# A stated order of 2997 steps: its first 950 rewritten with one filler product in place of ten, and three later steps moved forward

## The chip, the cores and the metric

The kernel runs on one core of a Trainium2 chip. The metric is the time of one execution on the device in microseconds. Before the change the median of three runs was 504.3 us (503.45 to 507.28). The core has five instruction streams that matter here: PE (TensorE, matrix products), DVE (VectorE), ACT (ScalarE), POOL (GpSimd) and SP (SyncE, which here only issues transfers). Each works off its own stream in order, and an instruction waits until what it needs is there.

## The reference

Two blocks follow one another. The first is a delta-rule recurrence over 768 tokens for 4 x 8 = 32 heads of width 48; the second, over the 384 features of each token, is a layer norm, a two-layer MLP with a relu, and a residual.

```python
k_n = k / (norm(k) + 1e-6)
state = zeros((B, H, D, D))
for t in range(S):
    y[:, :, t] = q[:, :, t] @ state
    v_old = state^T k_n[:, :, t]
    state = state + beta[t] * outer(k_n[:, :, t], v[:, :, t] - v_old)
x  = y as (B, S, H * D)                      # (4, 768, 384)
xn = (x - mean) / sqrt(var + 1e-6) * g_ln
out = x + relu(xn @ w_ch1) @ w_ch2           # 384 -> 1536 -> 384
```

All inputs and the output are float32.

## The kernel before

The 768 tokens are taken in 12 chunks of 64. Within a chunk the recurrence is turned into products: the products of the chunk's keys with one another (L772), the inverse of a triangular 64x64 matrix for each head, and then a handful of products with the state (`recur`, L970 to L1116), which is carried from chunk to chunk. The MLP of a chunk (`mlp`, L1275) follows its recurrence.

**The inverse.** For the first chunk it is built by doubling on PE (`first_inverse`, L643 to L750). For n = 1 to 5 there is a product E_n (L719) and a product Z_n (L738), each in two halves of 32 small products (half 0 and half 1 of the heads). Between E_n and Z_n a masked copy on DVE (`copy_predicated`, L728) puts E_n's result into place. Between Z_n and E_(n+1) DVE transposes the result (`nat`, L684) and ACT copies it (`back`, L678). For the other chunks the inverse is built on DVE in row blocks (L815 to L872, the pairs at L857 and L864) and joined by products on PE (`join`, L880 and after, products at L895 and L901).

**The recurrence of the first chunk.** u (product at L997, difference on DVE at L1002) and y (L1021) again come in two halves. ACT copies y into x (L1059), then the layer norm follows (statistics L941, normalisation L950, transposition on PE L1093, scaling by g_ln on ACT L1108). For later chunks the scaling by the reciprocal deviation is at L964 (DVE) and L966 (ACT).

**The MLP.** Chunk 0 is taken by halves of 128 columns (`by_halves`): first product L1323, second L1338. For chunks 1 to 3 the first product is at L1297, its relu on ACT at L1306. From chunk 4 the first product is replaced by fifteen smaller ones (`fifteen`, products L1218, sums L1234 to L1240). The second product is done by a scheme with seven products instead of eight (`seven`, L1399): products L1420, combinations of the relu's outputs on POOL (`comb`, L1407), sums on DVE (L1438).

**The weights** come as 64-bit words in pieces of 768 KB through ACT's queue (`fetch`), and are put together by two ACT instructions (L521, L529), one on DVE (L526) and one on POOL (`convert`, L539).

**What sets the order.** Building the kernel only records steps: `Line.add` stores for each of 2997 steps a function that issues its instructions, and which earlier steps it depends on. A string, `ORDER`, states in which order the steps are issued. `emit` reads it, asserts that a step's dependencies were issued, and calls the function. `in_this_order` then ties each engine's instructions into that order, and the transfers issued by SP and ACT into one order across both queues. No planner runs: what stands in `ORDER` is what each engine does. A step number a:b stands for a to b.

The letters z, y, x and w in `ORDER` are no steps of the computation. Each calls `zeros`, which issues one product of the identity with a broadcast column, 128 x 256, into the unused half of a bank; nothing reads it:

```python
    free = (f_[0], two[:, 0], by[:, 0], f_[1])

    def zeros(n):
        nc.tensor.matmul(free[n][:, 256:512], ident, ident[:, 0:1].to_broadcast([128, 256]))
```

Apart from them three products on zeros (`fill`, steps 71 to 73, L554) stand at the start.

The steps that the change names singly: 1026 and 1024 are two of chunk 2's first products of the MLP (L1297), 1027 and 1025 their relus (L1306); 993 is the layer-norm scaling on ACT (L966) and 994 the transposition on DVE behind it; 2953 and 2936 are two combinations on POOL (L1407) of the last chunk. In the front part: 59 is the load of g_ln, 69 and 386 are fetches of weight pieces, 360 is the second half of y of chunk 0.

Of the kernel before, what the change touches and what calls it, by code (L numbers as in the profile page):

```python
# [59 lines left out]
51 47 6 8 7 50 52 44 62 5 0 71:73 9:11 13 2 27 15 24 63 49 12 42 36 251 57 40 58 37 74 77 78 48 32 34 35 33 81 88 1 14 30 82 76 16 89 75 64 54 55 53  # L60
56 61 60 68 83 79 84 80 90 85 86 23 20 87 91 95 3 110 92 111 18 93 29 112 94 96 31 116 117 211 209 210 21 118 4 22 17 26 97 98 z 99 100 114 113 101
122 x 221 66 223 z 102 119 121 115 19 123:128 70 103 69 120 104 208 235 132 131 137 129 135 130 136 25 138 106 107 233 67 108 109 w 28 222 139 133 134
140 141 234 142:144 y 145 146 150 242 215 153 147 243 156 155 149 213 65 212 224 38 39 41 59 43 z 45 236 675 46 204 205 152 151 157 214 158 252 216
148 154 244 159 206 160:162 168 164 207 z 169 163 174 105 254 253 256 255 237 240 238 257 171:173 332 414 334 331 333 343 166 165 167 225 227 239 245
677 241 258 170 175 259 176 260 177 180 178 261 226 179 263 181 381 183 231 386 217 186 191 190 184 185 219 189 182 229 246 262 264:266 218 267:269 y
192 193 187 w 270:272 188 273 230 274:276 196 247 277 198 199 197 248 336 338 355 194 335 382 337 384 z 228 220 249 419 346 425 418 413 195 356 359
# [1585 lines left out]
```

## Time and profile before

| | us |
|---|---|
| median of three runs | 504.3 |
| lowest, highest | 503.45, 507.28 |
| profiled execution, its own time | 504.98 |
| its span in the profile | 502.8 |
| mean granted clock of PE in it | 0.981 |

Times in the profile count from the start of the span. A row of a timeline gives start, length, engine, line of the kernel, operation, tiles and shapes, and the number of like instructions in a row; in brackets stands the idle time of the engine ahead of it and what ended that. In a table by stretches each engine has its busy time and, in brackets, its number of instructions; then follow the granted clock of PE (1.00 is full), the share of the DMA engines and the bytes moved. A wait is put down to what came last. A product of fp32 leaves two records on PE where its tiles are 128 wide.

### The profile page before, as it was taken

The numbers are of one execution on the slowest core, as the hardware profiler recorded it, in microseconds if no ns is written. First come the engines' busy times: TensorE is split into PE (matmuls) and PEld (weight loads), VectorE is DVE, ScalarE is ACT, GpSimd is POOL, SyncE is SP. The second block draws the span as 40 slices with busy tenths as digits, with TensorE's granted clock in tenths as the row PEclk, the third lists the DMA queues.
The fourth block names the chain that finished last, engine by engine and source line by source line (L and its number), as shares of the span: only waits on it lengthen the run. The fifth ranks groups of instructions, "written<-read, shape, count | busy, mean of one in ns | idle before, by whom it ended". The sixth has DMA issues, their size and how long they took to land.

```text
span 502.8 us, 22213 instructions
## 1 busy us (share of the span) xinstructions
PE 488.1 (97%) x9624; PEld 445.3 (89%) x9624; DVE 348.5 (69%) x780; ACT 247.4 (49%) x620; POOL 277.8 (55%) x430
## 2 busy tenths in 40 slices
PE   8789999999999899999999999999999999999996
PEld 4567987689888898999999999999999999999996
DVE  6667998994889559886559898488899238143251
ACT  6767772623646234636544554436563347363230
POOL 5554468227873694629893561690642951645633
PEclk9976999999999999999999999999999999999999
DMA  9987987568656576448724525765234412111101
GB/s 166 308 153 187 252 200 103 78 178 130 84 91 108 186 128 112 68 78 214 153 36 66 108 48 162 145 92 83 75 68 126 94 22 60 44 50 47 26 15 31
DMA packets 196098, 54.99 MB, mean 109 GB/s; under 512 B 186077, under 2 KB 189405, under 8 KB 196001
## 3 DMA queue, kind: packets, MB, share of 16 engines
q1 hardware_dynamic: 189920, 40.58, 42.1%
q10 hardware_dynamic: 3872, 9.83, 6.3%
q0 software_dynamic: 2208, 3.17, 3.7%
q8 instruction: 75, 1.23, 1.0%
q14 instruction: 23, 0.18, 0.1%
HBM read 36.64 MB, written 16.91 MB: 107 GB/s over the span
## 4 chain that ended last, share of the span: by engine, by line
PE 81%; DVE 7%; DMA 4%; issue 3%; POOL 2%; ACT 1%; SPq 1%; DVEq 0%; ACTq 0%; POOLq 0%
PE f L1420 30%; PE f L1218 22%; PE f L1297 6%; DVE tmp L857 2%; DVE xb L864 2%; PE by L1021 2%; PE two L1014 2%; PE by L980 2%; PE two L980 2%; PE by L772 2%; PE f L1338 2%; PE two L1031 1%; PE two L772 1%; DMA gd<-gsb 1%; SPq L346 1%
## 5 line engine op out<-in xcount | busy, mean ns | idle before, releaser
L1407 POOL TENSOR_TENSOR h_all<-h_all 128x256 f32<-128x256 f32 x123 | 90.0, 744 | 131.6 <-PE f L1420 115.6
L1420 PE MATMUL f<-w_sb,h_all 128*128 128x192 f32 x492 | 108.1, 331 | 0.0
L1420 PE MATMUL f<-words,h_all 128*128 128x192 f32 x396 | 84.1, 330 | 1.7 <-ACT h_all L1306 1.4
L1420 PEld LDWEIGHTS f<-w_sb,h_all 128*128 128x128 f32 x492 | 81.7, 190 | 1.7 <-DVE o L1438 0.2
L857 DVE TENSOR_TENSOR tmp<-xb,gb 128x87 f32<-128x87 f32 (+21 forms) x186 | 74.1, 398 | 5.0
L864 DVE TENSOR_TENSOR xb<-xb,tmp 128x87 f32<-128x87 f32 (+21 forms) x186 | 72.3, 389 | 4.8
L1238 DVE TENSOR_TENSOR h_all<-h_all,f 128x512 f32<-128x512 f32 x96 | 63.4, 682 | 14.5 <-PE f L1218 13.3
L1420 PEld LDWEIGHTS f<-words,h_all 128*128 128x128 f32 x396 | 66.5, 190 | 3.2 <-ACT h_all L1306 1.5
L1297 PE MATMUL f<-xnt,w_sb 128*128 128x256 f32 x216 | 50.1, 382 | 0.0
L346 POOL DMA_DIRECT2D tb<-in_k_dram x64 | 41.8, 657 | 11.4 <-DVE kt L752 10.8
L1240 ACT ACTIVATE h_all<-h_all 128x512 f32<-128x512 f32 x48 | 28.4, 624 | 34.8 <-DVE h_all L1238 34.7
L1297 PEld LDWEIGHTS f<-xnt,w_sb 128*128 128x128 f32 x216 | 40.2, 190 | 5.1
L1234 ACT COPY h_all<-f 128x512 f32<-128x512 f32 x48 | 26.3, 590 | 34.9 <-PE f L1218 18.2
L1438 DVE TENSOR_TENSOR o<-f,x 128x192 f32<-128x192 f32 x33 | 11.6, 352 | 39.3 <-PE f L1420 22.8
L1218 PE MATMUL f<-words,w_sb 128*128 128x128 f32 x256 | 31.7, 276 | 0.0
L1218 PEld LDWEIGHTS f<-words,w_sb 128*128 128x128 f32 x256 | 30.0, 192 | 0.2
L1306 ACT ACTIVATE h_all<-f 128x256 f32<-128x256 f32 x36 | 13.4, 382 | 32.1 <-PE f L1297 31.9
L539 POOL TENSOR_TENSOR w_sb<-words 128x768 uint32<-128x768 uint32 (+1 forms) x11 | 15.2, 1387 | 19.9 <-DVE words L526 6.2
L1218 PE MATMUL f<-xnt,w_sb 128*128 128x128 f32 x192 | 25.4, 276 | 0.0
L1218 PEld LDWEIGHTS f<-xnt,w_sb 128*128 128x128 f32 x192 | 23.7, 192 | 0.1
L1438 DVE TENSOR_TENSOR o<-f,words 128x192 f32<-128x192 f32 x11 | 3.8, 349 | 25.4 <-PE f L1420 18.4
L1085 ACT ACTIVATE xnt<-xnt,g_sb 128x256 f32<-128x256 f32 x27 | 12.5, 499 | 16.4 <-DMA xnt<-xld 16.4
(250 smaller groups left out, 966.5 us busy)
## 6 DMA issues: line engine op xcount, KB each, us to landing
words<-in_moe_w_ch_dram ACTq DMA_DIRECT2D x10, 768.0 KB, 6.6
gd<-gsb SPq DMA_DIRECT2D x11, 512.0 KB, 3.8
v<-in_v_dram SPq DMA_DIRECT2D x24, 192.0 KB, 3.9
kr<-in_k_dram SPq DMA_DIRECT2D x46, 96.0 KB, 3.5
out_dram<-o SPq DMA_DIRECT2D x44, 96.0 KB, 2.4
xld<-xlt SPq DMA_DIRECT2D x9, 384.0 KB, 2.9
xnt<-xld SPq DMA_DIRECT2D x36, 96.0 KB, 3.1
gb<-gd SPq DMA_DIRECT2D x44, 64.0 KB, 3.2
```

The lines of the kernel that those rows point to most:

```text
L346: add(eng, cost, lambda: QUEUE[eng].dma_start(out=out_, in_=in_), r, w, bulk=n * ns / 16e3, **kw)
L857: lambda j=j, n=n, w=w, t=t: nc.vector.tensor_tensor(out=t, in0=xv[:, 0:n, j : j + 1].to_broadcast([np_, n, w]), in1=gv[:, j : j + 1, j + ...
L864: "DVE", dve(n * w), lambda t=t, rest=rest: nc.vector.tensor_tensor(out=rest, in0=rest, in1=t, op=ALU.subtract),
L980: nc.tensor.matmul(dst[half(e), hp, j], src[drows(hp), (e if n else key_half(c, hp, e)) * GP + j], s_all[drows(hp), e, j], start=(n == 0 o ...
L1218: nc.tensor.matmul(wide(p[:, 128 * n : 128 * n + 128]), w[n // 2][:, n % 2 * 128 : n % 2 * 128 + 128], r, start=start and n == 0, stop=Tru ...
L1234: add("ACT", act(512), lambda: nc.scalar.copy(o, p), pk, ok)
L1238: add("DVE", dve(512), lambda: nc.vector.tensor_tensor(out=o, in0=o, in1=p, op=op), pk, ok)
L1240: add("ACT", act(512), lambda: nc.scalar.activation(o, o, ACTF.Relu), [], ok)
L1297: nc.tensor.matmul(p[:, 0:TOK], w1_sb[:, t, f * 128 : (f + 1) * 128], xnt[:, t], start=(t == 0), stop=(t == KC - 1))
L1407: add(eng, cost, lambda: e.tensor_tensor(out=out_, in0=x, in1=y, op=op), r, w, port=2 if eng == "Pool" else 1, pr=-2)
L1420: lambda f=f, t=start and f == 0: nc.tensor.matmul(p[:, 0:D2], lhs(f), rhs[:, f], start=t, stop=(f == F2 - 1), skip_group_check=True),
L1438: lambda: e.tensor_tensor(out=out_, in0=a, in1=b_, op=ALU.add), r, w, pr=pr,
```

## The change

Only the string `ORDER` changes. No step is added or taken away; the letters are.

- The first 950 steps or so (up to about 140 us of the profile before) stand in another order, on all engines and all queues.
- The ten letters z x z w y z z y z z are replaced by a single y, between steps 97 and 98.
- Steps 1027, 1024 and 1025 stand ahead of 993 and 994 instead of behind them.
- Step 2953 stands ahead of 2936 instead of behind it.

All other lines of the string are the same in content, though its line breaks fall elsewhere at first. The beginning of the string before and after, the place of the relus, and the place of the combination:

```diff
-51 47 6 8 7 50 52 44 62 5 0 71:73 9:11 13 2 27 15 24 63 49 12 42 36 251 57 40 58 37 74 77 78 48 32 34 35 33 81 88 1 14 30 82 76 16 89 75 64 54 55 53
-56 61 60 68 83 79 84 80 90 85 86 23 20 87 91 95 3 110 92 111 18 93 29 112 94 96 31 116 117 211 209 210 21 118 4 22 17 26 97 98 z 99 100 114 113 101
-122 x 221 66 223 z 102 119 121 115 19 123:128 70 103 69 120 104 208 235 132 131 137 129 135 130 136 25 138 106 107 233 67 108 109 w 28 222 139 133 134
-140 141 234 142:144 y 145 146 150 242 215 153 147 243 156 155 149 213 65 212 224 38 39 41 59 43 z 45 236 675 46 204 205 152 151 157 214 158 252 216
-148 154 244 159 206 160:162 168 164 207 z 169 163 174 105 254 253 256 255 237 240 238 257 171:173 332 414 334 331 333 343 166 165 167 225 227 239 245
...
+51 52 63 62 6 9 8 5 47 71 72 58 10 11 13 1 3 12 14 27 0 7 74 76 4 49 42 40 36 38 43 37 73 50 48 32 34 78 77 33 81 88 64 55 56 54 53 60 61 68 82 89 75
+23 83 84 17 79 90 85 26 15 86 29 91 87 95 92 110 16 111 93 80 96 112 94 116:118 18 19 97 211 35 209 210 y 99 113 114 98 100 101 122 124 102 66 223 235
+119 221 120 70 115 121 103 208 104 123 20 24 125 21 126 25 127 128 132 135 129 136 130 131 137 69 138 222 107 106 22 139 30 140 144 213 67 147 233 109
+108 133 134 145 146 141:143 156 150 214 2 151 234 152 242 215 149 155 148 154 153 238 244 65 224 212 39 44 45 251 57 46 41 204 205 157 158 243 206 31
+162 239 28 159 160 164 161 168 163 236 216 207 170 169 174:176 245 105 253 256 255 254 240 237 167 166 165 231 257 171 172 217 225 241 180 381 183 173
...
-1390 1019 764 1108 985 765 949 1023 1034 1391 766 1230 986 767 948 1109 768 769 1388 1037 770 987 771 1110 1026 772 773 992 774 775 993 994 1038 776
-1027 1024 995 1670 1044 1231 996 1030 1120 1265 1025 1275 1047 1035 1121 1039 1064 1040 1048 1122 1045 780 1041 1032 777 1049 1033 778 1065 1042 1036
+1391 766 1230 986 767 948 1109 768 769 1388 1037 770 987 771 1110 1026 772 773 992 774 775 1027 1024 1025 993 994 1038 776 995 1670 1044 1231 996 1030
...
-2938 2928 2918 2933 2939 2929 2934 2940 2930 2952 2941 2931 2942 2935 2943 2945 2936 2944 2965 2946 2953 2966 2958 2937 2967 2947 2954 2968 2959 2969
+2930 2952 2941 2931 2942 2935 2943 2945 2953 2936 2944 2965 2946 2966 2958 2937 2967 2947 2954 2968 2959 2969 2948 2970 2960 2971 2949 2961 2972 2973
```

More of the change, by code (lines that the diff above doesn't have):

```diff
@@ L59 @@
 ORDER = """
-51 47 6 8 7 50 52 44 62 5 0 71:73 9:11 13 2 27 15 24 63 49 12 42 36 251 57 40 58 37 74 77 78 48 32 34 35 33 81 88 1 14 30 82 76 16 89 75 64 54 55 53
-56 61 60 68 83 79 84 80 90 85 86 23 20 87 91 95 3 110 92 111 18 93 29 112 94 96 31 116 117 211 209 210 21 118 4 22 17 26 97 98 z 99 100 114 113 101
-122 x 221 66 223 z 102 119 121 115 19 123:128 70 103 69 120 104 208 235 132 131 137 129 135 130 136 25 138 106 107 233 67 108 109 w 28 222 139 133 134
-140 141 234 142:144 y 145 146 150 242 215 153 147 243 156 155 149 213 65 212 224 38 39 41 59 43 z 45 236 675 46 204 205 152 151 157 214 158 252 216
-148 154 244 159 206 160:162 168 164 207 z 169 163 174 105 254 253 256 255 237 240 238 257 171:173 332 414 334 331 333 343 166 165 167 225 227 239 245
-677 241 258 170 175 259 176 260 177 180 178 261 226 179 263 181 381 183 231 386 217 186 191 190 184 185 219 189 182 229 246 262 264:266 218 267:269 y
-192 193 187 w 270:272 188 273 230 274:276 196 247 277 198 199 197 248 336 338 355 194 335 382 337 384 z 228 220 249 419 346 425 418 413 195 356 359
[83 rows of a table removed]
+51 52 63 62 6 9 8 5 47 71 72 58 10 11 13 1 3 12 14 27 0 7 74 76 4 49 42 40 36 38 43 37 73 50 48 32 34 78 77 33 81 88 64 55 56 54 53 60 61 68 82 89 75
+23 83 84 17 79 90 85 26 15 86 29 91 87 95 92 110 16 111 93 80 96 112 94 116:118 18 19 97 211 35 209 210 y 99 113 114 98 100 101 122 124 102 66 223 235
[88 rows of a table added]
 """
```

163 rows, old and new, of the table ORDER are left out of this document.

## Prediction

> **What bounds the kernel now.** I read the page first, then the busy time by stretches, the waits of TensorE, and the timelines of the places that the change touches. The page's first part, its row of the clock, and the first two lines of the chain that ended last:
>
> ```profile
> PE 488.1 (97%) x9624; PEld 445.3 (89%) x9624; DVE 348.5 (69%) x780; ACT 247.4 (49%) x620; POOL 277.8 (55%) x430
> PEclk9976999999999999999999999999999999999999
> PE 81%; DVE 7%; DMA 4%; issue 3%; POOL 2%; ACT 1%; SPq 1%; DVEq 0%; ACTq 0%; POOLq 0%
> ```
>
> PE is busy for 488.1 of 502.8 us and makes 81% of the chain. So only two things can shorten this kernel: less PE time, or less of the 14.7 us in which PE is idle. Where the idle time lies, the busy time by stretches shows (columns: length, busy us of each engine, granted clock, DMA share, GB/s):
>
> ```profile
> 0.00:10.00 10.00, 7.75 (x86) 3.96 (x87) 5.33 (x28) 6.22 (x14) 6.66 (x18) 1.00 0.89 139
> 10.00:20.00 10.00, 8.55 (x248) 6.88 (x248) 8.62 (x27) 8.48 (x23) 2.40 (x3) 1.00 1.11 257
> 20.00:30.00 10.00, 7.75 (x262) 6.13 (x260) 5.07 (x16) 6.03 (x15) 7.62 (x12) 0.83 0.78 253
> 30.00:40.00 10.00, 7.82 (x181) 5.88 (x173) 7.71 (x26) 5.96 (x19) 5.09 (x5) 0.67 1.01 216
> 40.00:50.00 10.00, 9.79 (x269) 8.11 (x270) 6.93 (x22) 7.29 (x19) 4.31 (x5) 0.65 0.73 152
> 50.00:110.00 60.00, 59.43 (x1160) 48.03 (x1162) 54.95 (x131) 35.74 (x97) 28.65 (x35) 1.00 0.74 163
> 160.00:170.00 10.00, 8.60 (x219) 7.37 (x218) 9.48 (x24) 5.00 (x13) 3.92 (x6) 1.00 0.32 87
> 170.00:490.00 320.00, 320.00 (x6040) 306.58 (x6038) 209.98 (x427) 150.03 (x360) 179.56 (x290) 1.00 0.44 89
> ```
>
> In the first 50 us PE is idle for 8.3 us, in 160 to 170 for 1.40 us, in 170 to 490 not at all. The first 50 us are the inverse of the first chunk: doubling steps E1, Z1, ... E5, Z5, each a group of 32 small products per half, with a DVE or ACT copy between one and the next. There the zeros stand too. The rest of the idle time lies ahead of the first product or at the very end.
>
> **The change part by part.** (1) The two relus. On PE and ACT around 167 us (columns: start, length, engine, line, operation, count, idle time before and its releaser):
>
> ```profile
> 166.27 0.59 PE L1297 MATMUL f<-xnt,w_sb 128*128 128x256 f32 x2
> 166.80 1.16 PE L772 MATMUL two<-kt 48*64 48x64 f32 x64
> 169.36 0.59 PE L1420 MATMUL f<-words,h_all 128*128 128x192 f32 x2 [1.40 <-ACT h_all L1306]
> 168.43 0.62 ACT L966 ACTIVATE xln<-xln,rstd 128x384 f32<-128x384 f32 x1 [2.94 <-DVE rstd L964]
> 168.95 0.64 ACT L1306 ACTIVATE h_all<-f 128x256 f32<-128x256 f32 x2
> ```
>
> The product that the relus read ends at 166.27 + 0.59 = 166.86. ACT is free, but the layer-norm scaling (step 993, L966) stands ahead of them and waits 2.94 us for DVE, so the relus run only at 168.95, and PE stands still from 167.96 to 169.36. With both relus ahead of 993 they would run from about 166.9 to 167.55 (166.86 + 0.64, and a little for the release), before PE has finished the 64 products at 167.96. The whole 1.40 goes. Behind them, 993 starts when DVE releases it at 168.43, as before, so nobody waits for ACT longer. What is late next: PE then runs 1.4 us closer to DVE, which is busy for 9.48 of 10 us there. If half of it came back as a later wait the term would be 0.7; I find the work behind 169.36 (the sums and combinations of this chunk) released by PE itself, and take −1.40. Ends: −0.7 and −1.40.
>
> (2) The GpSimd combination near the end (step 2953 ahead of 2936):
>
> ```profile
> 485.45 6.44 POOL L1407 TENSOR_TENSOR h_all<-h_all 128x256 f32<-128x256 f32 x9 [11.49 <-PE f L1420]
> 490.46 0.59 PE L1420 MATMUL f<-words,h_all 128*128 128x192 f32 x2 [0.28 <-POOL h_all L1407]
> ```
>
> POOL runs nine combinations without a gap until 491.89. Exchanging two of them takes away the wait of 0.28 for the first, but the last still ends at 491.89, and PE reaches the products that need the later ones at about the same moment. The wait moves on. I take 0; ends −0.28 and +0.28.
>
> (3) The zeros. Nine of ten go. One row of the zeros' line (ns min/median/max, first and last start), and the busy time by the stretches of the granted clock:
>
> ```profile
> L1514 PE MATMUL two<-ident x4: 634/713/793, 24.2 to 39.3; 128*128 128x256 f32 x4
> 23.20:26.60 3.40, 3.40 (x88) 0.50 0.78 291
> 26.60:33.40 6.80, 4.75 (x188) 1.00 0.82 193
> 33.40:47.10 13.70, 13.44 (x271) 0.50 0.85 165
> ```
>
> A zeros product costs time only where a useful step is ready behind it. Three places, each with the DVE row that made the step ready:
>
> ```profile
> 23.36 0.49 DVE L728 COPY_PREDICATED gsb<-u,by 128x128 f32<-128x128 int32 x2 [2.13 <-PE by L719]
> 23.13 1.09 PE L738 MATMUL f<-xt,gsb 64*64 64x64 f32 x29
> 25.30 1.13 PE L738 MATMUL by<-xt,gsb 64*64 64x64 f32 x32
> 38.00 0.77 DVE L684 STREAM_TRANSPOSE qt<-f 128x256 f32<-128x256 f32 x2
> 39.83 1.08 PE L719 MATMUL two<-qt,gsb 64*64 64x32 f32 x32
> 40.98 0.45 DVE L728 COPY_PREDICATED pt<-u,two 128x256 f32<-128x256 int32 x1 [0.72 <-PE two L719]
> 41.99 1.08 PE L738 MATMUL f<-xt,pt 64*64 64x32 f32 x32
> ```
>
> Z2's second half was ready at 23.85 (23.36 + 0.49), PE free at 24.22, and it started at 25.30: 1.08 lost. E5's operand was there at 38.77, it started at 39.83: 1.06. Z5 was ready at 41.43 and started at 41.99: 0.56. Together −2.70. The other zeros I cost at nothing: PE waits behind them for DVE, ACT or its own instructions anyway, as these rows show:
>
> ```profile
> 12.93 0.70 PE L1514 MATMUL by<-ident 128*128 128x256 f32 x2
> 16.12 0.34 PE L719 MATMUL by<-qt,gsb 64*64 64x64 f32 x7 [1.04 <-issue]
> 17.97 0.67 PE L719 MATMUL two<-qt,gsb 64*64 64x32 f32 x32
> 19.54 0.70 PE L1514 MATMUL f<-ident 128*128 128x256 f32 x2
> 20.72 0.42 PE L719 MATMUL by<-qt,gsb 64*64 64x32 f32 x13 [0.47 <-DVE qt L684]
> 22.78 0.48 PE L719 MATMUL by<-qt,gsb 64*64 64x32 f32 x18 [1.64 <-issue]
> ```
>
> The stalls put down to issue I expect to stay: they come at even distances in PE's stream of instructions, and taking out two for each of nine zeros only moves them by a step. Zero, from −1.6 to +1.6 (one such stall hidden or laid open).
>
> Against the gain stands the clock. It is full in 26.60 to 33.40, right behind the stretch with the zeros that begin at 24.2, and half around it. Without them I expect that stretch at half clock as well. Price: a group of 32 products takes 0.67 at full clock (17.97) and 1.08 at half (39.83), 0.41 more; E3 and Z3, four groups, lie on the path there: +1.64. Ends: 0 (the clock is as before) and 188 of 32 times 0.41 = +2.4 (every record of the stretch).
>
> The Trainium skill ("TensorE: Matmul & The Clock Gate", Part 1, What's actually happening) says that the gate watches a free-running window of some 3.4 us and goes to full after one busy window. By that rule the short gaps that the zeros filled would not decide, the term would be 0 and the time 1.64 lower. The trace does not bear it out: PE was busy for 13.44 of 13.70 us in 33.40 to 47.10 and stayed at half, so I keep the term.
>
> (4) The further order of the first 950 steps. It has the same instructions, all engines and both DMA queues in another order. Two things I can see to cost: ACT's back copies of one half of Z3 and Z4 now stand behind the other half's, so that E4's and Z4's second groups start some 1.5 to 2 us later, in the cover of E5's first; and the second half of the first output (step 360) waits for a DVE step put back by four places, past a pair that is slow while POOL converts:
>
> ```profile
> 51.73 1.19 DVE L864 TENSOR_TENSOR xb<-xb,tmp 64x231 f32<-64x231 f32 x1
> 52.95 0.40 DVE L857 TENSOR_TENSOR tmp<-xb,gb 64x240 f32<-64x240 f32 x1
> ```
>
> One such clash is 1.19 − 0.40 = 0.8. I take +0.6, between 0 and 1.2 (one clash and one more step of 0.4 ahead). The transfers that move (the weight pieces from about 15 to 21 us and from 37 to 44 us, g_ln's to about 43 us) still land ahead of their use at about 50 us by my count; POOL's loads of keys move forward, past nothing that waits. Zero; if g_ln were late, the first transposes of the MLP would wait up to about 1 us.
>
> (5) What the front's gain meets next. From 50 to 110 us DVE is busy for 54.95 of 60.00 us, and PE steps start within a tenth or two of their DVE operand:
>
> ```profile
> 83.10 0.75 PE L895 MATMUL f<-xnj,gsb 32*32 32x32 f32 x64 [0.16 <-DVE xnj L885]
> 97.15 0.55 PE L1093 MATMUL by<-ident,xln 128*128 128x128 f32 x3
> ```
>
> This chain begins with what the front hands over at 47 to 51 us, so a shorter front moves it as a whole, and the new order puts some DVE work (differences of weights, a reciprocal) behind it. I pass the front's gain on in full.
>
> **The sum.** Front: −2.70 + 1.64 + 0.6 = −0.46. Relus −1.40, combination 0, transfers 0. In all −1.86, against the profiled execution's own 504.98 us: 503.1. The median of the runs shown is 504.3, 0.7 below that execution, so against the median the forecast is 504.3 − 1.86 = 502.4 us.
>
> **The rivals.** A: the zeros are worth all that they occupy on the chain. The chain of the first 56 us, by line, says how much that is:
>
> ```profile
> by line: issue 12.2%; DMA kr<-in_k_dram 8.7%; PE by L738 7.6%; PE by L719 6.6%; PE f L1514 6.1%; PE two L719 5.9%; PE f L565 5.6%; PE f L738 5.3%; PE f L772 5.1%; DVE xb L864 4.2%; PE two L1514 4.1%; ACT xt L678 3.1%; DVE tmp L857 2.6%; PE
> ```
>
> 6.1% and 4.1% of 56 are 5.7 us. With the relus: 504.3 − 5.7 − 1.4 = 497.2 us. It asks that the clock holds and that the further order fills the waits. For it speaks that the whole front was reordered; against it, the copies between the groups, which no order shortens. With the skill's rule alone (term of the clock at 0) it comes half way, to 500.8.
>
> B: the front's gain is hidden behind DVE in 50 to 110 us, because the DVE work of the inverse of chunk 1 started no earlier. Only the relus remain: 504.3 − 1.40 = 502.9 us. For it speaks 54.95 of 60.00; against it, that this DVE work starts with the front's own operands.
>
> C, on the other side: without zeros the clock is released later, in the dense phase behind 47.10, where PE is busy for nearly all of the time. A window is 3.40 us by the rows of the clock (13.70 is four of them). Each further window at half clock there delivers half its work: 1.7 us lost. From two windows on (502.4 + 3.4 = 505.8) the kernel is slower than before; four, a stretch as long as 33.40 to 47.10, give 502.4 + 6.8 = 509.2. For it speaks that those four windows stayed at half with PE busy; against it, that the full-size products of the MLP begin at 51 us, and the clock never fell after that.
>
> **How the numbers follow.** The measurement of this kernel tells about 1% from no change, so "same" reaches from 499.3 to 509.3. Chances: the forecast, 501 to 504, 0.45; A 0.20, nearly all of it below 499.3; B 0.20, inside "same" and inside the forecast's own range; C 0.15, of which somewhat over half passes 509.3, since other mishaps of a new order (a late transfer, one more issue stall of 1.6) would come on top. So faster 0.19, same 0.72, slower 0.09. The range leaves out half of A and half of C: 498.2 to 508.0.
>
> **What would show it.** Relus: no wait of PE for L1306 near 166 us. Clock: the row of granted clock in 23 to 47 us at half throughout, full from 47 to 50; full in 26 to 33 would say A, half behind 50 would say C. Front: E5's first group at about 38 instead of 39.83, the first MLP product (51.49 before) at 50.6 to 51.4. Combination: PE's wait for L1407 moved to about 491.9. If the first MLP product comes later than 51.5, part (4) was mis-sized, and the prediction stands only on the relus.

## The result and the profile after

The changed kernel took 508.2 us in the median of 20 runs (505.7 to 514.7), the kernel before 505.16 us in 20 runs (502.78 to 508.33). The ratio is 1.0071, interval 1.0048 to 1.0095: some 3.6 us slower. The forecast was 502.4, the range 498.2 to 508.0. By the 1% that the prediction takes for no change, the kernel stayed the same, which had the chance of 0.72; but the sign was wrong, and the time lies just outside the range. Runs that were visibly disturbed are left out of the ratios and of the means below.

The profiled execution took 506.78 us, 1.80 more than that of before (504.98). The page, its first part, the clock, and the first line of the chain that ended last:

```profile
PE 481.7 (95%) x9606; PEld 443.6 (88%) x9606; DVE 346.4 (69%) x780; ACT 249.0 (49%) x620; POOL 278.1 (55%) x430
...
PEclk9856999999999999999999999999999999999999
...
PE 80%; DVE 9%; DMA 4%; issue 3%; SPq 2%; POOL 1%; ACT 1%; DVEq 0%; ACTq 0%; POOLq 0%
```

PE is busy for 6.4 us less (above all the zeros are gone), yet the span is longer: PE's idle time rose from 14.7 us to 23.4. Where, the busy time by stretches of the changed kernel says:

```profile
10.00:20.00 10.00, 7.13 (x260) 5.97 (x259) 8.32 (x24) 8.38 (x22) 2.34 (x3) 1.00 1.15 296
20.00:30.00 10.00, 6.22 (x237) 5.79 (x236) 5.14 (x16) 6.54 (x14) 6.82 (x11) 0.63 0.98 295
30.00:40.00 10.00, 6.09 (x164) 5.33 (x168) 7.88 (x25) 6.08 (x17) 4.42 (x4) 0.50 0.93 182
40.00:50.00 10.00, 8.15 (x267) 7.52 (x267) 9.20 (x26) 6.62 (x18) 6.92 (x8) 0.67 0.49 123
50.00:110.00 60.00, 57.75 (x1087) 47.12 (x1086) 51.58 (x123) 35.45 (x95) 30.53 (x38) 1.00 0.76 166
...
160.00:170.00 10.00, 10.00 (x198) 8.64 (x194) 8.53 (x26) 6.84 (x21) 1.09 (x2) 1.00 0.53 119
170.00:490.00 320.00, 319.89 (x6085) 306.34 (x6075) 210.31 (x426) 151.28 (x361) 181.66 (x293) 1.00 0.43 88
```

Three things are to be seen. Between 20 and 40 us the clock is at 0.63 and 0.50 where it was 0.83 and 0.67. In 50 to 110 us, which were all but full before (59.43), PE is idle for 2.25 us. And the gap in 160 to 170 is gone. The same time by the stretches of the clock, PE alone:

```profile
5.60:22.70 17.10, 12.35 (x428) 1.00 1.16 290
22.70:46.60 23.90, 16.17 (x462) 0.50 0.79 187
46.60:60.00 13.40, 10.55 (x305) 1.00 0.67 149
```

One stretch of 23.90 us at half clock, seven windows, where before had 3.40 and 13.70. The timeline of PE at the places where it now stands still, or that the prediction named (start, length, and in brackets the idle time and its releaser):

```profile
26.76 1.44 PE L772 MATMUL f<-qt,kt 48*64 48x64 f32 x43 [2.53 <-issue]
...
38.34 1.07 PE L719 MATMUL two<-qt,gsb 64*64 64x32 f32 x30 [0.21 <-DVE qt L684]
...
50.81 1.61 PE L1323 MATMUL f<-xnt,w_sb 128*128 128x128 f32 x12
...
53.36 0.68 PE L1021 MATMUL by<-u,pt 64*64 64x48 f32 x32 [0.94 <-DVE u L1002]
...
55.70 0.51 PE L1031 MATMUL two<-u,kr 64*64 64x48 f32 x20 [1.31 <-issue]
...
123.72 0.75 PE L895 MATMUL f<-xnj,gsb 32*32 32x32 f32 x64 [1.31 <-DVE xnj L885]
```

Up to the first MLP product the forecast holds: it starts at 50.81 (51.49 before; forecast 50.6 to 51.4), E5's first group at 38 (39.83 before). Then come three waits that before did not have, 0.94, 1.31 and 1.31 us. "issue" means that PE waited for nothing that the profile shows. It is read here as its own instructions. Counted in the traces, such stalls stand behind record 221, 347, 475, 602 and 1111 of PE's stream in this kernel, 126 to 128 apart or a multiple of that. In all 20 profiles of this study they fall on the same series of counts, to within two records, whatever step stands there (of the later ones 2640, 2768 and 4172 come more than once). On the instruction queue, the page of the changed kernel lists 75 packets (1.23 MB in all, 16 KB each) for the 2 x 9606 records of PE and PEld, about one for each 128 products with their loads, and in the front such a packet starts 2.5 to 3.1 us before PE goes on:

```profile
q8 instruction: 75, 1.23, 1.0%
```

The relus and the tail of the changed kernel, PE's timeline:

```profile
169.56 1.16 PE L772 MATMUL two<-kt 48*64 48x64 f32 x64
170.65 0.59 PE L1420 MATMUL f<-words,h_all 128*128 128x192 f32 x2
...
493.76 0.59 PE L1420 MATMUL f<-words,h_all 128*128 128x192 f32 x2 [0.71 <-POOL h_all L1407]
```

PE no longer waits for the relus. Of the combinations, the wait of 0.28 us has become one of 0.71, four products later.

Followed step by step in both traces, PE's lag behind the kernel before is -0.68 us at the first MLP product, +1.19 at the join of chunk 1 (84.29 against 83.10), +2.76 from 146 to 168 us, +1.29 behind the relus, +1.43 at 200 us, +1.57 at 491 us and +1.81 at the end.

### The profile page after: what moved, and what is told of

It reads as the page before. It is cut to its first block, busy times and chain, and to the rows that moved or that the text cites. A ratio compares the mean times of both kernels' runs of the same rounds, so it can differ in the third digit from the quotient of the medians.

```text
span 505.1 us, 22181 instructions
## 1 busy us (share of the span) xinstructions
PE 481.7 (95%) x9606; PEld 443.6 (88%) x9606; DVE 346.4 (69%) x780; ACT 249.0 (49%) x620; POOL 278.1 (55%) x430
## 3 DMA queue, kind: packets, MB, share of 16 engines
q8 instruction: 75, 1.23, 1.0%
## 4 chain that ended last, share of the span: by engine, by line
PE 80%; DVE 9%; DMA 4%; issue 3%; SPq 2%; POOL 1%; ACT 1%; DVEq 0%; ACTq 0%; POOLq 0%
PE f L1420 30%; PE f L1218 22%; PE f L1297 6%; DVE xb L864 2%; DVE tmp L857 2%; PE by L1021 2%; PE by L980 2%; PE two L1014 2%; PE by L772 2%; PE two L980 2%; SPq L346 2%; PE two L1031 2%; PE two L772 1%; DMA gd<-gsb 1%; POOL h_all L1407 1%
## 5 line engine op out<-in xcount | busy, mean ns | idle before, releaser
L864 DVE TENSOR_TENSOR xb<-xb,tmp 128x87 f32<-128x87 f32 (+21 forms) x186 | 74.7, 401 | 4.8
L857 DVE TENSOR_TENSOR tmp<-xb,gb 128x87 f32<-128x87 f32 (+21 forms) x186 | 69.7, 375 | 5.0
L1297 PE MATMUL f<-xnt,w_sb 128*128 128x256 f32 x216 | 50.1, 383 | 0.0
L1297 PEld LDWEIGHTS f<-xnt,w_sb 128*128 128x128 f32 x216 | 40.2, 190 | 5.2
L1234 ACT COPY h_all<-f 128x512 f32<-128x512 f32 x48 | 26.2, 589 | 34.0 <-PE f L1218 17.3
L1438 DVE TENSOR_TENSOR o<-f,x 128x192 f32<-128x192 f32 x33 | 11.4, 352 | 38.3 <-PE f L1420 24.1
L1306 ACT ACTIVATE h_all<-f 128x256 f32<-128x256 f32 x36 | 13.4, 383 | 34.8 <-PE f L1297 32.6
L1085 ACT ACTIVATE xnt<-xnt,g_sb 128x256 f32<-128x256 f32 x27 | 12.5, 499 | 19.4 <-DMA xnt<-xld 18.6
L1438 DVE TENSOR_TENSOR o<-f,words 128x192 f32<-128x192 f32 x11 | 3.9, 353 | 25.4 <-PE f L1420 18.3
```

Source lines behind the costliest of these rows:

```text
L857: lambda j=j, n=n, w=w, t=t: nc.vector.tensor_tensor(out=t, in0=xv[:, 0:n, j : j + 1].to_broadcast([np_, n, w]), in1=gv[:, j : j + 1, j + ...
L864: "DVE", dve(n * w), lambda t=t, rest=rest: nc.vector.tensor_tensor(out=rest, in0=rest, in1=t, op=ALU.subtract),
L1234: add("ACT", act(512), lambda: nc.scalar.copy(o, p), pk, ok)
L1297: nc.tensor.matmul(p[:, 0:TOK], w1_sb[:, t, f * 128 : (f + 1) * 128], xnt[:, t], start=(t == 0), stop=(t == KC - 1))
```

## The experiments

Seventeen kernels were run, one of them twice, in five rounds, each against the kernel before on the same chip. Beside the ratio, two figures of each kernel are used: the mean time at half clock of its runs (from each run's granted clock and span: 2 x (1 - clock) x span), and the sum of PE's waits put down to issue in its profile. In 113 runs of the kernel before, the time at half clock varied from 3 to 24 us, 14.3 in the mean, and the run was longer by 0.19 us for each us of it (a straight line through them; correlation 0.57). In the changed kernel's own runs it is 0.34 us for each us (19 runs, from 20 to 41 us at half clock; correlation 0.88). The 20 runs of before beside the changed kernel have no clock on record, so the 14.3 stand for them.

Runs of both kernels with the same time at half clock can be set side by side. With 20 to 25 us of it, 8 runs of the changed kernel took 506.7 us in the mean, and 17 runs of before, from the five rounds, 506.2. So at a like clock some 0.5 us of the 3.6 are left; most of the loss goes with the clock. These are runs of different rounds, whose means for the kernel before lie between 503.3 and 505.2 us, so the 0.5 is known to about 1 us.

| kernel | ratio to before (interval) | half clock, us | issue, us |
|---|---|---|---|
| before | 1 | 14.3 | 4.9 |
| changed | 1.0071 (1.0048 to 1.0095) | 27.7 | 6.7 |
| x1_relus, and again | 1.0005 (0.9982 to 1.0027), 0.9981 (0.9951 to 1.0012) | 17.3, 14.9 | 3.8, 4.6 |
| x2_front | 1.0064 (1.0034 to 1.0095) | 26.6 | 6.4 |
| x3_nine_zeros_out | 1.0057 (1.0028 to 1.0087) | 29.4 | 7.1 |
| y4_three_kept (four zeros) | 1.0045 (1.0014 to 1.0075) | 24.8 | 4.6 |
| y3_three_out (seven zeros) | 1.0019 (0.9991 to 1.0047) | 19.6 | 4.2 |
| x4_ten_zeros_in | 1.0136 (1.0089 to 1.0184) | 20.4 | 4.0 |
| y1_dve_gap | 1.0076 (1.0049 to 1.0103) | 27.8 | 5.4 |
| y2_zeros_in_waits | 1.0090 (1.0054 to 1.0126) | 18.9 | 6.4 |
| z1_zeros_and_spread | 1.0070 (1.0049 to 1.0091) | 22.4 | 4.0 |
| z2_front_filled | 1.0071 (1.0035 to 1.0107) | 27.4 | 3.3 |
| z3_zeros_doubled | 1.0139 (1.0083 to 1.0194) | 9.6 | 9.9 |
| z4_transfers_order | 1.0112 (1.0067 to 1.0157) | 20.7 | 2.3 |
| w1_narrow_zeros | 1.0023 (0.9991 to 1.0055) | 32.5 | 2.1 |
| w2_after_narrow | 1.0174 (1.0120 to 1.0229) | 32.2 | 10.7 |
| w3_doubled_narrow | 1.0118 (1.0068 to 1.0167) | 11.2 | 9.3 |
| u1_after_4_narrow | 1.0103 (1.0058 to 1.0147) | 28.8 | 8.1 |
| u2_after_16_narrow | 1.0304 (1.0254 to 1.0353) | 42.5 | 10.3 |

**The parts alone.** The relus, twice:

```diff
-... 773 992 774 775 993 994 1038 776 1027 1024 995 ... 1265 1025 1275
+... 773 992 774 775 1027 1024 1025 993 994 1038 776 995 ... 1265 1275
```

> The kernel before with steps 1027, 1024, 1025 moved ahead of 993, nothing else. Theory: PE's wait of 1.40 us near 168 us goes and nothing takes its place: 1.4 us below before (in the changed kernel the lag of PE's steps fell from 2.76 us to 1.29 us at this place). Rival: the time comes back as a later wait of PE for DVE or POOL, and the difference is under 0.7 us.

> The kernel before with the two relus moved forward alone, once more: the first time it stood 0.3 us below before, with an interval of 1.1 us to either side, and 0.9 us below at the same time at half clock. Theory: 0.5 to 1.4 us below before. Rival: no difference beyond 0.4 us.

The first run stands 0.25 us above before, the second 0.96 below, each within its interval of about 1.1 to 1.6 us; together some 0.4 us below. That is less than the 1.4, and then the 0.5 to 1.4, that the two theories named, and not apart from zero. The wait itself is gone, as PE's timeline of the first shows:

```profile
167.87 1.16 PE L772 MATMUL two<-kt 48*64 48x64 f32 x64
168.96 0.59 PE L1420 MATMUL f<-words,h_all 128*128 128x192 f32 x2
```

Followed step by step, PE in the first profile is 1.07 us later than in the kernel before when it reaches the place, and 0.40 earlier when it leaves it; in the second it is 2.78 us earlier and then 4.25. So in each profile 1.47 us go at the place, about as forecast; on the whole time the runs do not tell a gain of up to some 1.3 us from none.

The front, with the relus and the combination in their old places (the changed kernel's first 940 steps, then the old order):

> The kernel before with the changed kernel's first 940 steps (with its one zeros product), relus and combination in their old places. Theory: the whole loss is in the front, some 2.8 us by the lag of PE's steps at 150 us in the changed kernel's profile, of which the relus give 1.4 back later; here nothing is given back, so 2.5 to 3.5 us above before. Rival (the loss lies at the end, with the combination): 0 to 1 us above before.

It stands 3.2 us above before, inside what was expected (2.5 to 3.5). So the loss lies in the front. But the expectation also had the moved relus give 1.4 us back, and the changed kernel, which has them moved, stands no lower (3.6). ACT's timeline at that place, and PE's:

```profile
168.56 0.62 ACT L966 ACTIVATE xln<-xln,rstd 128x384 f32<-128x384 f32 x1 [1.41 <-DVE rstd L964]
```

```profile
169.86 1.16 PE L772 MATMUL two<-kt 48*64 48x64 f32 x64
170.95 0.59 PE L1420 MATMUL f<-words,h_all 128*128 128x192 f32 x2
```

The relus stand in their old place and PE does not wait for them. PE's 64 products come at 169.86, 3.06 us later than before, but the release by DVE that ACT waits for comes at 168.56 against 168.43. A late PE finds the relus done. So in this front the wait of 1.40 us is gone without the move: PE is 3.06 us late ahead of the place and 1.58 behind it. The wait soaks up 1.4 us of a lateness, with the relus moved or not; the 1.4 are saved once, and in this front not by the move.

**The zeros in the old order.** Nine out; then three out; then six out. The letters of the old order, what stays (the ninth letter of before is a w, where the list of the change above has a z):

```diff
 before              z x z w y z z y w z
+x3_nine_zeros_out   z
+y4_three_kept       z . . . y . . y w .
+y3_three_out        z x z w . z z . . z
```

> The kernel before in its own order with nine of its ten zeros products taken out (the first stays). Theory A, the order is what costs: the zeros' own time and the colder clock about cancel in the front, the time is within 0.7 us of before, on either side. Theory B, the missing zeros cost by the clock: 2 to 3 us above before, with the granted clock at half from about 23 to 47 us and beyond. Theory C, the zeros were worth their 2.7 us: 2 to 3 us below before.

> The kernel before with three of its ten zeros products taken out, those that the prediction priced at 2.7 us because a step stood ready behind them (ahead of the second half of Z2, of E5 and of Z5). If the prediction's price holds and the other seven keep the clock: 1.5 to 2.7 us below before. If these three are what keeps the clock up: 0 to 3 us above, with the granted clock below 0.98.

> The kernel before with six of its ten zeros products taken out, those that cover waits; the first and the three that delay a ready step stay. If the covering zeros keep the clock: 2 to 3 us above before, like the kernel with nine out. If the three do: within 1 us of before.

With one, four, seven and ten zeros the time at half clock is 29.4, 24.8, 19.6 and 14.3 us, and the time 2.9, 2.3, 1.0 and 0 us above before. Theory B's number came for the nine. The six that cover waits cost 2.3 us when they went, and the three that the prediction priced at 2.7 us gained nothing (1.0 above, from 0.5 below to 2.4 above). So the clock goes with the number of zeros rather than with one kind of them. The profiled runs of the first and the last of these, PE, granted clock:

```profile
30.00:40.00 10.00, 6.16 (x182) 0.50 0.82 140
40.00:50.00 10.00, 8.56 (x232) 0.50 0.65 165
50.00:60.00 10.00, 9.63 (x197) 0.73 0.69 177
```

```profile
30.00:40.00 10.00, 8.33 (x216) 0.56 0.95 198
40.00:50.00 10.00, 9.73 (x213) 0.50 0.67 128
50.00:60.00 10.00, 9.63 (x183) 0.91 0.72 196
```

The first three rows are of the kernel with nine out: half clock reaches into the dense products behind 50 us, to 0.73 in the mean of 50 to 60 (that execution was the slowest of its twelve). The last three are of the one with three out.

The clock is not all of it. Followed step by step, the kernel with three out stands 0.76 us ahead of before at 145 us, and 1.45 ahead behind the relus at 169; so its front did gain. By 195 us it is 0.61 behind, after waits of 0.37 us for ACT (L1085) and 1.17 for DVE's sums (L1438) ahead of first products of the MLP (L1297) that before does not have. The kernel with nine out has such waits of 1.13 and 0.77 us there. No run took them away, so how much of these losses is the clock's stays open.

**The zeros in the new order.** Ten behind the same PE steps as before; then nine, eight of them ahead of PE steps that waited 0.44 to 1.24 us:

```diff
-x2 and changed      y only
+x4_ten_zeros_in     98 z 100 101 122 x z 124 ... 107 w 106 ... 144 y 213 ... 156 z 150 ... 168 z 163 ... 192 w 268 ... 186 y 219 ... 335 z 195
+y2_zeros_in_waits   y 99 ... z 124 ... y 138 ... y 156 ... y 168 ... z 180 ... y 177 ... z 186 ... y 194
```

> The changed kernel with ten zeros products behind the same PE steps as in the kernel before, in place of its one. Theory A: within 0.7 us of the changed kernel, so 1 to 2.5 us above before. Theory B: the clock comes back and with it 2 to 3 us, at or below before. Theory C: the products add some 2 us more, 4 us or more above before.

> The changed kernel with eight more zeros products, each ahead of a PE step of the first inverse that waited 0.44 to 1.24 us for DVE or ACT, in a bank that nobody reads then. Theory clock: the mean granted clock rises from 0.972 to that of before (0.983 or more), and the time comes down by 0.25 to 0.37 us for each us less at half clock, some 2 to 4 us, to within 1 us of before. Rival (the order is the loss): the clock rises, but the time stays 2 us or more above before, or rises as it did with ten zeros behind the old steps.

In both the clock came back (half clock 20.4 and 18.9 us against 27.7) and the time rose, to 6.9 and 4.5 us above before. By the numbers that is theory C for the first, and the rival for the second, that the order is the loss. In both profiles PE no longer waits at the join near 123 us; it stands still a little later, as this row of y2 shows:

```profile
137.60 0.48 PE L1420 MATMUL f<-words,h_all 128*128 128x192 f32 x2 [2.42 <-issue]
```

In x4 the stall of 2.03 us ends at 134.11, and behind it the clock falls to half for 3.4 us, among products that leave PE hardly any idle time. PE's and the other engines' busy time by stretches, with the clock in the third column from the end:

```profile
130.00:134.00 4.00, 2.08 (x150) 1.74 (x141) 2.71 (x9) 3.48 (x12) 1.64 (x4) 0.99 0.66 83
134.00:138.00 4.00, 3.89 (x14) 3.90 (x15) 0.36 (x1) 1.19 (x4) 1.77 (x3) 0.58 0.48 73
```

The same is in the traces of five other versions: 3.4 us at half from 201.7 (z3), 142.7 (z4), 131.3 (u1), and 143.0 and 156.7 (u2), and 6.8 from 138.9 (w2), each within about 2 us of the end of a wait of 1.5 to 3.1 us. It does not follow each such wait (y2's 2.42 and w3's 2.36 have none). With PE busy throughout, 3.4 us at half clock would be 1.7 us of lost work, as the prediction's rival C reckons. What it held against itself, that the clock never fell again behind 51 us, is true of before and of the changed kernel up to their last 5 us, and not of these.

The stall in y2 was put to the test by setting three groups of small products apart:

```diff
-828 ... 832 833 830 834 ... 716 578 918 919 910 920 924 925
+828 ... 832 833 918 919 830 834 ... 716 910 920 924 578 925
```

> The kernel with eight more zeros in the changed order (y2_zeros_in_waits), and besides three PE steps of many small products (s of chunk 2, and the join of chunk 3) set apart by products of the MLP, where PE stood still for 2.42 us with nothing to wait for but its own instructions (near 137 us). Theory instructions: PE runs through 192 small products in 3 us and its instructions do not come as fast; set apart, that stall falls below 1.2 us and the time comes down by 1 to 2 us, to 2 to 3.5 us above before. Rival: the stall moves to another place, and the time stays 4 us or more above before.

```profile
138.73 0.26 PE L895 MATMUL f<-xnj,gsb 32*32 32x32 f32 x8 [0.41 <-issue]
```

The stall fell from 2.42 to 0.41 us and the time from 4.5 to 3.5 us above before. The stall can be taken away by mixing long products in; the gain of 1.0 is within the two intervals together.

**The waits of the new order.** DVE's steps 666 and 372 put back to where DVE was idle; and the two waits behind the first MLP product filled:

```diff
 y1_dve_gap
-... 449 371 636 ... 509 372 510 ... 519 666 520 ...
+... 449 371 372 666 636 ... 509 510 ... 519 520 ...
 z2_front_filled (PE)
-590 588 360 379 594 592 347 348 598
+590 588 347 360 592 348 379 594 598
```

> The changed kernel with two DVE steps put back into DVE's idle time near 79 us: the difference of weights 666 (0.75 us) and the reciprocal 372 (0.16 us), which the new order had put into the chain of the next inverse. Theory D (the wait of 1.31 us at 123.7 us is made of these): PE's wait there falls to about 0.4, and the time is 0.5 to 1 us below the changed kernel, 1.5 to 3 us above before. Rival (the clock is all): no difference to the changed kernel beyond 0.5 us, 3 us above before.

> The changed kernel with the two waits behind its first MLP product filled: the transposes 347 in front of the second half of y (wait of 0.94 us for DVE), and 592 and 348 between it and s (stall of 1.31 us), and the same three steps set apart as in z1. Theory order: these two waits are part of the loss, the time comes down by 1 to 2 us, to 1 to 2.5 us above before. Rival (the chain through DVE and the transfers to the next join at 123.7 us takes the place): PE waits longer there, the time stays at 3 to 4 us above before.

Both theories fell, and the rivals' numbers came. With the steps put back PE waited no less at the join of chunk 2, and with the front filled (the waits of 0.94 and 1.31 became 0.33 and nothing) it still waited there. PE's rows at that place, y1 first:

```profile
125.03 0.75 PE L895 MATMUL f<-xnj,gsb 32*32 32x32 f32 x64 [1.61 <-DVE xnj L885]
```

```profile
122.13 0.75 PE L895 MATMUL f<-xnj,gsb 32*32 32x32 f32 x64 [1.49 <-DVE xnj L885]
```

In the ratios neither moved from the changed kernel (1.0076 and 1.0071). What feeds that join can be followed backwards. DVE works on chunk 2's row blocks from 84.50 to 113.5 us with hardly a gap, then they are stored and loaded again. That work waits its turn behind chunk 1's join on DVE, and chunk 1's join ends a chain that begins with a product of keys on PE (63.39 in the changed kernel, 63.30 before) and goes over a store, SP's queue and two loads. The longest pieces of it in the changed kernel (start, length):

```profile
65.75 6.34 DMA gd<-gsb
...
77.76 1.90 SPq L346
...
79.70 2.01 DMA xt<-xd
...
83.11 0.70 DVE xnj L885
```

The same chain in the kernel before:

```profile
65.81 5.58 DMA gd<-gsb
...
75.68 0.48 SPq L346
...
76.21 3.46 DMA gb<-gd
...
82.35 0.71 DVE xnj L885
```

The product starts within 0.1 us of its old time, although the first MLP product came 0.68 us earlier; the store takes 0.76 us longer, SP issues on this chain until 79.66 where it was done at 76.16, and DVE's transposition comes 0.76 us later. PE's join of chunk 2 is then at 123.72 where it was at 122.60. In the profile of z2 the product comes at 61.34, and both joins move with it (82.51 and 122.13); the wait stays, since PE too is earlier. That execution took 505.01 us, 1.77 less than the changed kernel's, which its median of 12 runs does not repeat. The reading that fits is that PE work that comes early gains here only as far as the keys' product comes early with it; no run moved that product alone.

**The transfers' order alone.** The old order on PE, DVE and ACT, the new one on SP and POOL:

> The kernel before, with its ten zeros and its own order on PE, DVE and ACT, and the changed kernel's order on SP and POOL alone (transfers and POOL's steps of the first 940). If the changed order's own cost lies in its transfers: 1.5 us or more above before. If it lies with PE, DVE and ACT: within 0.8 us of before.

```profile
140.60 0.75 PE L895 MATMUL f<-xnj,gsb 32*32 32x32 f32 x64 [3.13 <-DVE xnj L885]
```

It stands 5.6 us above before, with a wait of 3.13 us at the join of chunk 3. The mixture costs more than the whole new order, so it says only that POOL's and SP's places matter here by several us, not which half of the changed kernel's loss is theirs.

**Work or number.** More zeros, and zeros without most of their work:

```diff
 z3_zeros_doubled:   zz xx zz ww yy zz zz yy ww zz in the places of before
 w1, w2, w3:
+        w = 1 if len(issued) in small else 256
+        nc.tensor.matmul(free[n][:, 256 : 256 + w], ident, ident[:, 0:1].to_broadcast([128, w]))
```

In w1 all but the first of the ten are narrow. In w3 a narrow one stands behind each of the ten. In w2, u1 and u2 nine, four and sixteen narrow ones stand behind the changed kernel's single y.

> The kernel before with each of its ten zeros products issued twice. From 1 to 4 to 7 to 10 zeros in the order of before the mean time at half clock fell from 29 to 25, 20 and 13 to 15 us, and the time by 2.6 us. If the clock goes on rising: half clock for under 10 us, time 0 to 1 us below before. If ten are enough: the same clock, and the added products delay steps, 1 to 3 us above before.

> The kernel before with nine of its ten zeros products made one column wide in place of 256: PE's instructions keep their number and places, their work goes. Theory clock: as with the nine taken out, 2 to 3.5 us above before, with a mean granted clock of about 0.971. Rival (instruction places): taking products out moved the points at which PE waits for its own instructions, and that was the loss; then within 0.8 us of before, although the clock falls.

> The kernel before with one more zeros product of one column behind each of its ten: as many PE instructions as with ten zeros doubled, which stood 8 us above before at a higher clock, but not their work. If that loss came from the places of the instructions (stalls of 2.80 and 1.45 us near 200 and 145 us in its profile): 4 us or more above before here too. If it came from the work of the zeros: within 1 us of before.

w1 keeps the number of PE's instructions and takes their work: 32.5 us at half clock, colder than with nine out, and the time 1.2 us above before (from 0.5 below to 2.8 above). That is between the two expectations and decides for neither, and the interval overlaps that of x3 (1.4 to 4.4). Its profile has few stalls (2.1 us), and of the waits near 190 us only 0.2.

z3 and w3 have the best clock of all, 9.6 and 11.2 us at half, and stand 7.0 and 6.0 us above before. Their order is that of before, letter for letter, from the front on. w3's front was early: PE is busy without a gap from 50 to 110 us. The loss comes after. The row of w3, and that of before:

```profile
110.00:210.00 100.00, 93.83 (x2135) 1.00 0.61 109
```

```profile
110.00:210.00 100.00, 98.22 (x2226) 1.00 0.65 116
```

and the waits of PE in w3 in that stretch (us in total, times, longest):

```profile
PE f L895 <- issue: 2.4, 1, 2.4
PE f L1297 <- DVE o L1438: 2.0, 1, 2.0
PE by L772 <- issue: 1.0, 1, 1.0
PE f L901 <- issue: 0.8, 1, 0.8
```

Before has 0.4 of issue there, at another step, and the 1.40 for the relus; w3 has not that one, and 1.96 for DVE's sums (L1438) near 192 us in its place. So of 4.4 us the issue stalls make 3.8. In z3 the stalls fall on the same three steps, 2.80, 1.45 and 0.65 us, with and without the work of the added zeros. z3 besides loses its early front at 83.12 us, in a wait of 1.83 for DVE at the join of chunk 1, and has 3.4 us at half clock behind the stall near 200. With ten products more ahead of them, which are 20 records of PE's stream, the counts at which PE waits for its next instructions fall on other steps: in the middle of groups of 64 small products (L895, L772), which PE runs through in about a microsecond. So w3 and before, alike in order and w3 with the better clock, differ by 4.4 us in this stretch, and the place of these points explains most of it; no run moved them without adding or taking out products, so this stays the reading that fits, not a thing shown by itself.

> The changed kernel with nine zeros products of one column behind its one zeros product, which moves all later PE instructions by as many places as in the kernel before, and adds hardly any work. Theory clock: as the changed kernel, 2.5 to 4 us above before. Rival (instruction places): the stalls of the changed kernel go elsewhere, and the time differs from it by 1.5 us or more, up or down.

> The changed kernel with four narrow products behind its one zeros product: all later PE instructions move by 8 places, no work to speak of is added. Nine of them cost 5 us against the changed kernel. If the places of the instructions set the stalls: 1 us or more away from the changed kernel (which stood 3.5 us above before), below or above, with the sum of PE's waits for its own instructions (6.7 us in the changed kernel's profile, 10.7 with nine) moving the same way. If those 5 us had another cause that grows with the count: between, at 5 to 6 us above before.

> The changed kernel with sixteen narrow products behind its one zeros product. If the cost grows with the count: 10 us or more above before. If it is the places: below that of nine (8.8 us above before), and with the sum of PE's waits for its own instructions in the profile as the measure.

These were meant to add nothing but places, and that premise was wrong. The sixteen of u2 stand at the head of the first inverse and take

```profile
12.14 4.07 PE L1519 MATMUL two<-ident 128*128 128x256 f32 x34
```

4.07 us with the one wide product (0.60), about 0.2 each; u1, w2 and u2 stand 5.2, 8.8 and 15.3 us above before, where the changed kernel stands 3.6. In their profiles the added products take about 1.3 (u1, at half clock there), 1.9 and 3.5 us, against 1.6, 5.2 and 11.7 us above the changed kernel. Where more is lost, colder clock (28.8, 32.2 and 42.5 us at half, some of it in the dense part) and longer issue waits stand beside it; no run parts them. The two readings of the expectation are not told apart by them, since the cost rose with the number, and part of it was work.

## Why the prediction was wrong

**What failed, in short.** The profiled pair can be followed in order of time. Up to the first MLP product the sum holds: PE comes 0.68 us earlier, with 0.46 forecast. Then the step fails that passes the front's gain on in full with 0.6 us for new waits: by 146 us PE is 2.76 us late, 3.44 us lost. At the relus 1.47 come back, as the sum has it, and behind them 0.5 is lost by the end: +1.81. The second step that failed is the size of the clock's term: the pair differs by 6 us at half clock, about what was forecast, but the runs in the mean by 13.4.

**Relus (-1.40): the number came, the move did not earn it.** The wait vanished wherever the move was made, and also in the front alone, where it was not. In the changed front PE reaches the place 2.76 us late, and the wait would have taken 1.4 us off that lateness with the relus in their old place. So the -1.40 stands once in the sum; that it came out with a late front is luck, since the prediction had PE come early there.

**Combination (0): right within its bounds on time, wrong on the wait.** The wait moved on, as said, but grew, and PE's lag grew by 0.24 us there. In the nine profiles with the step moved the wait is 0.69 to 0.72 us, in the eleven without it 0.27 to 0.30.

**Zeros (-2.70) and clock (+1.64).** That the clock would fall was foreseen, with its place: half throughout 23 to 47 us. The profiled pair bears this out, and the front came out at -0.68 at the first MLP product, with -0.46 forecast. What failed is the size: one stretch of 6.8 us was counted, read off one profiled execution. Over the runs the time at half clock went from 14.3 to 27.7 us, 13.4 more; at 0.19 to 0.34 us each that is 2.6 to 4.6 us. Rival C named the loss, with half a us for each us at half clock, and only behind 50 us; the price measured is lower, probably because PE waits for part of the time at half clock anyway. The price of the zeros is not borne out by the time: with the three out that it names the kernel gained nothing, as told above. The Trainium skill ("TensorE: Matmul & The Clock Gate", Part 1, What's actually happening) has the gate release after one busy window and close after one idle window. The second agrees with the trace only if idle is taken loosely: in before, the stretches ahead of both drops held 1.28 and 1.48 us of PE work in 3.40. The first does not: half clock held on through 13.70 us in which PE was busy for 13.44.

```profile
19.80:23.20 3.40, 1.28 (x42) 1.00 0.94 370
30.00:33.40 3.40, 1.48 (x43) 1.00 1.03 292
```


**Issue stalls (0, from -1.6 to +1.6): a little outside the bound.** They were taken to stay as they were. In the changed kernel's profile they add up to 6.7 us against 4.9, 1.8 more; in three profiles of before's order, which differ in the relus alone, they are 3.8 to 4.9. That they come at even distances was right. What it costs when the points fall on other steps was put at one stall of 1.6 us; by w3's profile (3.8 us more) it can be more than twice that.

**Waits behind the front (+0.6, the rest passed on in full): wrong.** The wait for the second half of y came as foreseen, 0.94 us. The stall of 1.31 behind it and the wait of 1.31 at the join of chunk 2 did not. The prediction put the moved DVE work (a difference of weights, step 666, and a reciprocal) behind the chain; putting it back changed nothing (y1), so that was not the cause. The chain through the store, SP and DVE starts with a product that the new order did not move forward (63.39 against 63.30), and ends 0.76 us later. That is like rival B, a gain hidden behind DVE's chain, but the front was not only hidden: it ended later than before. The three waits less those of before at 52.69, 83.10 and 132.37 (3.56 less 0.37, 0.16 and 0.38) make 2.65 of the 3.44 lost; for the other 0.8 the profile shows no wait of PE, and filling two of the three (z2) did not bring the time down. What set the rest off stays open.

**The sum again**, from what was measured. The profiled pair: front -0.68, waits behind it +3.44, relus -1.47, the small rest and the combination +0.52, in all +1.81. The runs have 7.3 us more at half clock between them than this pair (13.4 against 6.1), which at 0.19 to 0.34 is 1.4 to 2.5 more: +3.2 to +4.3. Measured are 3.6, from 2.4 to 4.8. What the new order is worth at an equal clock is then little, about 0.5 us of loss by the runs set side by side above. No run gives it the clock of before without added products: ten zeros in it cost more than one.

Of the versions tried, the relus alone are the only one whose median lay below the kernel before, in both runs, and by less than can be told.

## What to carry to other kernels

Terms of a sum that lie one after the other on the same engine do not add: a wait further on absorbs lateness, so walk them in order of time. A product that fills a wait may be worth more by what it does to the clock than it costs, and one profiled execution shows one draw of that clock; look at the granted clock of all runs, and set runs of a like clock side by side. And where one engine runs through dense groups of small instructions, adding or removing any instruction ahead moves the steps at which it waits for its own code, and here a wait of about 2 us in a dense part was at times followed by a stretch at half clock.

## What the runs showed of the hardware

The time at half clock of one and the same kernel varies between 3 and 24 us from run to run, and more zeros bring it down steadily (29.4, 24.8, 19.6, 14.3, 9.6 us with 1, 4, 7, 10 and 20). PE's waits put down to issue fall on the same counts of its stream in all profiles; one reached 2.8 us in the dense part (z3), and they sum to 10.7 us in one execution (w2). In six versions the clock fell to half again in the dense part, for 3.4 or 6.8 us. A product of one column, 128 x 128, took about 0.2 us of PE's time, not nothing.
